# Attention and top-1 expert layer on one core: low halves and gating moved to VectorE, second-layer weight units cut by column parity, first expert loads on GpSimd's queue

## The chip, the cores and the metric

The kernel runs on 1 core of one Trainium2 chip. The metric is the device time of one execution in microseconds (us), as the median of several runs.

## The reference

For 8 batches of 448 tokens and 12 heads of 64 columns, sigmoid attention is computed. Its output, 3584 tokens by 768 columns, is the input of a layer of 8 experts of which each token takes one. All is float32.

```python
scores = scale * np.matmul(q, k.transpose(0, 1, 3, 2)) - np.log(S)
attn = 1.0 / (1.0 + np.exp(-scores))
x = np.matmul(attn, v)                    # per head; then tokens x 768
logits = x @ w_gate                       # 768 x 8
expert_idx = np.argmax(logits, axis=1)
gate_w = softmax(logits)[arange(N), expert_idx]
for e in range(E):
    mask = expert_idx == e
    h = np.maximum(x[mask] @ w1[e], 0.0)  # 768 x 1024
    out[mask] = gate_w[mask, None] * (h @ w2[e])   # 1024 x 768
```

## The kernel before

**Stages.** Attention runs over pairs of heads in 168 steps (`attention()`, L562). A step computes scores (`sc`, L522), their sigmoid on ScalarE (`at`, L509) and the product with the values (`av`, L536). From step 36 on, each step also runs 14 matmuls of the expert layer (`more`, L647): the generator `moe(b, wts)` (L192) yields after each matmul, so that attention and experts alternate on TensorE. A batch has 21 steps and 288 expert matmuls. When attention is done, some 300 expert matmuls are left; between them the kernel prepares a last stage.

**A batch and its expert.** For each batch the gate (`gate_a` to `gate_e`, L252 to L384) finds each token's expert and the expert that most of the batch's tokens chose, `ri`. `load_regs` (L386) reads `ri` into a register of SyncE, and `moe` sends the whole batch, 448 columns wide, through that one expert. Tokens with another expert are recorded in `recs` by four indirect DMAs on GpSimd's queue (L361), and are computed in the last stage, in items of up to 256 rows (`item`, L828), whose results overwrite those rows of the output.

**Split weights.** Each float32 factor is split in a high half (a rounded copy, made by ScalarE, L143) and a low half (factor minus high half, L144), and each product is made of three matmuls: high by high, high by low, low by high. `part_split(st, parts, eng)` (L141) makes both halves; `eng` makes the low one. For the batches that engine is GpSimd.

**Units and rings.** The first layer has 8 units per batch (`KF`), each 128 columns of w1, 128x768; a unit serves 18 matmuls. The second layer has 12 units (`NU`), each 128x512. Its output is made in three blocks `d` of 256 columns, and each block in two passes `t`, one for the even columns and one for the odd. A second-layer unit held two row blocks of w2 with all 256 columns, and the matmul took every second column of it as its weights (L223). So the four units of a block served pass 0, and again pass 1, and were given back one by one in pass 1. The ring of w2 units has 5 buffers, that of w1 units 3 (`RING`, L128). Raw weights come by DMA into a ring of 5 (`wst`, L162), all on SyncE's queue, which also loads q, k and most of v. One raw load of w2 (`w2_rows`, L133) holds four row blocks of 256 columns, that is two units.

**Order.** All of this is written in the order in which each engine gets it (`manual_schedule`), and each engine and each queue takes its instructions strictly in that order. `wts.ahead(n)` (L171) emits the splits up to unit n, and the raw loads that this allows. In the second layer it was called in pass 1 only, after every second row block (L233). After each pass VectorE transposes the pass's sum out of PSUM (`ob`, L237; two PSUM buffers, `ps_moe`); after both, GpSimd multiplies the block by the gates (L239), and its queue stores it by four DMAs (L244). `ob` has two buffers, which the last stage uses again for its `hf` (L900).

Of the kernel before, what the change touches and what calls it, by code (L numbers as in the profile page):

```python
# [19 lines left out]
P = 128  # L20
# [5 lines left out]
def tile_sigmoid_attention_top1_moe(  # L26
# [18 lines left out]
    nc = tc.nc  # L45
    B, H, S, D = q.shape
    NT, DM = out.shape
    E = w_gate.shape[1]
# [81 lines left out]
    def raw_view(st, n):  # L130
        return st.rearrange("p (t f) -> p t f", f=n)
# [9 lines left out]
    def part_split(st, parts, eng):  # L141
        hi, lo = parts
        nc.scalar.copy(hi, st)  # L143
        eng.tensor_tensor(lo, st, hi.bitcast(F32), op=ALU.subtract)  # L144

    class Weights:
# [9 lines left out]
        def load(self, n):  # L156
            while self.loaded < min(n, len(self.eregs) * self.LOADS):
                b, i = divmod(self.loaded, self.LOADS)
                ereg = self.eregs[b]()
                if ereg is None:  # L160
                    break
                st = wpool.tile([P, 1024], F32, tag="wst", bufs=RAWS_AHEAD, name=f"wst_{b}_{i}")  # L162
                if i < KF:
                    src = w1[bass.ds(ereg, 1), :, i * P : (i + 1) * P].rearrange("e (t p) f -> p (e t) f", p=P)
                    nc.sync.dma_start(raw_view(st[:, :DM], P), src)
                else:
                    w2_rows(ereg, i - KF, st)
                self.raw[self.loaded] = st
                self.loaded += 1

        def ahead(self, n):  # L171

            while True:
                b, i = divmod(self.split, self.PARTS)
                u = i - KF
                at = b * self.LOADS + (i if u < 0 else KF + u // 2)
                self.load(at + RAWS_AHEAD)
                if self.split >= n or at not in self.raw:
                    break
                st = self.raw[at]  # L180
                if u < 0:
                    parts = part_tiles("w1", DM, f"{b}_{i}")
                    part_split(st[:, :DM], parts, nc.gpsimd)
                else:
                    parts = part_tiles("w2", 512, f"{b}_{i}")
                    part_split(st[:, u % 2 * 512 : (u % 2 + 1) * 512], parts, nc.gpsimd)
                if u < 0 or u % 2:
                    del self.raw[at]
                self.parts[self.split] = parts
                self.split += 1  # L190

    def moe(b, wts):  # L192
# [25 lines left out]
        for d in range(ND):  # L218
            ob = opool.tile([P, NB, 32, 2], F32, tag="ob", name=f"ob_{b}_{d}")
            for t in range(2):  # L220
                ps = ps_moe.tile([P, 512], F32, tag="moe", name=f"ps2_{b}_{d}_{t}")
                for j in range(KF):
                    whi, wlo = (  # L223
                        x[:, j % 2 * DW : (j % 2 + 1) * DW].rearrange("p (m t) -> p t m", t=2)[:, t]
                        for x in wts.parts[w0 + KF + 4 * d + j // 2]
                    )
                    hh, hl = hts[j]
                    for n, (a, b_) in enumerate(((whi, hh), (whi, hl), (wlo, hh))):
                        nc.tensor.matmul(  # L229
                            ps[:, :S], a, b_, start=(j == 0 and n == 0), stop=(j == KF - 1 and n == 2)  # L230
                        )
                        yield
                    if t == 1 and j % 2:  # L233
                        wts.ahead(w0 + KF + min(NU, 4 * d + j // 2 + 6))
                    if d == ND - 1 and (t, j) in ((0, 1), (0, 5), (1, 1)):
                        wts.ahead(w0 + wts.PARTS + {(0, 1): 1, (0, 5): 2, (1, 1): 3}[t, j])
                nc.vector.transpose(ob[:, :, :, t], ps[:, :S].rearrange("p (j s) -> p j s", s=32))  # L237
            obv = ob.rearrange("p j s t -> p j (s t)")
            nc.gpsimd.tensor_tensor(  # L239
                obv, obv, gate_rows[b].unsqueeze(2).broadcast_to([P, NB, 2 * 32]), op=ALU.mult  # L240
            )
            for i in range(4):
# [143 lines left out]
    def load_regs(b):  # L386
        ri = gate_out[b]
        regs[b] = nc.sync.value_load(ri[0:1, 0:1], min_val=0, max_val=E - 1)

    KH = KD // 2  # L390
    xts = {}
# [170 lines left out]
    def attention():  # L562
# [31 lines left out]
        for s in range(N_ST + 11):  # L594
            u, i = divmod(s, ST)
            if s == 6:
                setup()
            if s == START - 1:
                wts.ahead(2)
            if s < ALONE:  # L600
                steps(s, 1, s - 1)
            elif i == 0:
# [360 lines left out]
```

## Time and profile before

| what | us |
|---|---|
| median of 3 runs | 889.35 (889.07 to 890.4) |
| the profiled execution | 887.08 |
| its span, first to last instruction | 885.1 |
| TensorE busy | 848.2 |
| VectorE, ScalarE, GpSimd busy | 300.1, 392.0, 410.3 |
| mean granted TensorE clock | 0.982 |

The busy time of an engine says little about an engine that others wait for only at some points. In the views of waits and groups, a row names the line, the engine, what is written and read, and how long the engine sat idle before it and for whom. "POOL" is GpSimd, "DVE" VectorE, "ACT" ScalarE, "PE" TensorE and "SPq" SyncE's queue. In the timeline a row has its start and its length; "x3" joins three instructions; the time in brackets is the idle time before it, with what ended it. Batches are counted from 0; the names `w2l_17` and the like in the orders below are numbered per batch: 0 to 7 are first-layer units, 8 to 19 second-layer units.

### The profile page before, as it was taken

How to read it: one execution, taken by the hardware profiler on the slowest of the kernel's cores; microseconds unless marked ns; L12 is line 12 of the kernel's file. 1: busy time of each engine (PE TensorE's matmuls, PEld its weight loads, DVE VectorE, ACT ScalarE, POOL GpSimd, SP SyncE). 2: the span in 40 equal slices, each digit the busy share in tenths (PEclk: the TensorE clock that was granted, in tenths of full speed). 3: DMA queues.
4: the chain of work that ended last, by engine and by line, in shares of the span. 5: the costliest groups of instructions: out<-in, count | busy, mean ns of one | idle time of the engine just before them, and what ended most of it. 6: DMA issues, size and time to landing. Idle time of an engine off the chain costs nothing.

```text
span 885.1 us, 15521 instructions
## 1 busy us (share of the span) xinstructions
PE 848.2 (96%) x5612; PEld 645.1 (73%) x5612; DVE 300.1 (34%) x679; ACT 392.0 (44%) x691; POOL 410.3 (46%) x377
## 2 busy tenths in 40 slices
PE   8998999999999999999989999899989998999986
PEld 6855678677687776677668677677767787899875
DVE  2453145123342235123422135022331135516354
ACT  4865543435433634444534534254335421234444
POOL 3114234744185326633464325724364448766340
PEclk8999999999999999999999999999999999899998
DMA  8788863675646844866446654668233424545614
GB/s 144 133 151 189 195 150 94 164 149 127 139 111 152 175 97 106 184 147 132 85 129 144 155 118 124 133 140 179 72 95 109 128 55 132 147 148 181 238 59 139
DMA packets 301929, 120.60 MB, mean 136 GB/s; under 512 B 211588, under 2 KB 296660, under 8 KB 301856
## 3 DMA queue, kind: packets, MB, share of 16 engines
q1 hardware_dynamic: 292512, 104.25, 50.1%
q0 software_dynamic: 7488, 14.93, 7.1%
q8 instruction: 44, 0.72, 0.4%
q10 hardware_dynamic: 1856, 0.46, 0.3%
q14 instruction: 29, 0.24, 0.1%
HBM read 97.55 MB, written 24.64 MB: 138 GB/s over the span
## 4 chain that ended last, share of the span: by engine, by line
PE 83%; issue 4%; DMA 4%; POOL 3%; DVE 2%; SPq 2%; ACT 1%; POOLq 0%; ACTq 0%; DVEq 0%
PE ps L208 27%; PE ps L229 23%; PE sc L522 13%; PE av L536 13%; PE ps L839 3%; PE psg L256 2%; POOL recs L361 1%; SPq L445 1%; DMA w2r<-in_moe_w_dram 1%; DMA first<-in_q_dram 1%; POOL w2l L144 1%; DMA out_dram<-ob 1%; DVE w1l_item L144 1%; SPq L408 1%; DMA wst<-in_moe_w_dram 0%
## 5 line engine op out<-in xcount | busy, mean ns | idle before, releaser
L509 ACT ACTIVATE at<-sc,bias_s 128x448 f32<-128x448 f32 x336 | 196.0, 636 | 198.8 <-PE sc L522 198.6
L144 POOL TENSOR_TENSOR w2l<-wst,w2h 128x512 fp32r<-128x512 f32 x96 | 121.5, 1291 | 161.8 <-ACT w2h L143 153.1
L522 PE MATMUL sc<-qt,kt 64*64 64x448 f32 x1344 | 177.0, 556 | 3.3 <-ACT at L509 2.5
L144 POOL TENSOR_TENSOR w1l<-wst,w1h 128x768 fp32r<-128x768 f32 x64 | 117.0, 1840 | 136.2 <-ACT w1h L143 123.1
L536 PE MATMUL av<-at,vn 64*64 64x448 f32 x1344 | 172.5, 544 | 0.0
L229 PE MATMUL ps<-hh,w2l 128*128 128x448 f32 x384 | 144.5, 376 | 12.2 <-POOL w2l L144 12.2
L208 PE MATMUL ps<-xh,w1l 128*128 128x448 f32 x384 | 142.1, 370 | 4.8 <-POOL w1l L144 4.8
L208 PE MATMUL ps<-xh,w1h 128*128 128x448 f32 x384 | 143.2, 373 | 0.0
L229 PE MATMUL ps<-hl,w2h 128*128 128x448 f32 x384 | 142.9, 372 | 0.0
L229 PE MATMUL ps<-hh,w2h 128*128 128x448 f32 x384 | 142.5, 371 | 0.0
L208 PE MATMUL ps<-xl,w1h 128*128 128x448 f32 x384 | 142.3, 370 | 0.0
L522 PEld LDWEIGHTS sc<-qt,kt 64*64 64x64 f32 x1344 | 77.8, 192 | 64.4 <-issue 50.2
L213 ACT ACTIVATE hh<-ps 128x448 fp32r<-128x448 f32 x64 | 35.1, 549 | 149.3 <-PE ps L208 149.3
L536 PEld LDWEIGHTS av<-at,vn 64*64 64x64 f32 x1344 | 55.6, 134 | 57.4 <-issue 55.1
L214 DVE SCALAR_TENSOR_TENSOR hl<-ps,hh 128x448 fp32r<-128x448 f32 x64 | 39.7, 620 | 166.5 <-ACT hh L213 166.5
L143 ACT CAST w2h<-wst 128x512 fp32r<-128x512 f32 x96 | 58.1, 624 | 80.3 <-PE ps L229 70.0
L229 PEld LDWEIGHTS ps<-hh,w2l 128*128 128x128 f32 x384 | 75.5, 197 | 24.7 <-POOL w2l L144 13.7
L208 PEld LDWEIGHTS ps<-xh,w1h 128*128 128x128 f32 x384 | 72.9, 190 | 16.6 <-issue 10.7
L208 PEld LDWEIGHTS ps<-xh,w1l 128*128 128x128 f32 x384 | 72.9, 190 | 12.9 <-POOL w1l L144 5.6
L229 PEld LDWEIGHTS ps<-hl,w2h 128*128 128x128 f32 x384 | 75.1, 196 | 9.2 <-issue 5.5
L208 PEld LDWEIGHTS ps<-xl,w1h 128*128 128x128 f32 x384 | 72.8, 190 | 8.8 <-issue 2.8
L229 PEld LDWEIGHTS ps<-hh,w2h 128*128 128x128 f32 x384 | 75.4, 196 | 3.5
(150 smaller groups left out, 817.8 us busy)
## 6 DMA issues: line engine op xcount, KB each, us to landing
wst<-in_moe_w_dram SPq DMA_DIRECT2D x64, 384.0 KB, 4.2
wst<-in_moe_w_dram SPq DMA_DIRECT2D x48, 512.0 KB, 4.1
x_tok<-xt SPq DMA_DIRECT2D x64, 168.0 KB, 3.9
out_dram<-ob POOLq DMA_DIRECT2D x96, 112.0 KB, 2.9
kn<-in_k_dram SPq DMA_DIRECT2D x184, 56.0 KB, 3.9
qn<-in_q_dram SPq DMA_DIRECT2D x184, 56.0 KB, 2.7
vn<-in_v_dram SPq DMA_DIRECT2D x76, 112.0 KB, 3.8
w1r<-in_moe_w_dram SPq DMA_DIRECT2D x12, 512.0 KB, 3.4
```

Of the source, the lines that this page charges most:

```text
L143: nc.scalar.copy(hi, st)
L144: eng.tensor_tensor(lo, st, hi.bitcast(F32), op=ALU.subtract)
L208: nc.tensor.matmul(ps[:, :S], a[:, ws], b_, start=(t == 0 and n == 0), stop=(t == KD - 1 and n == 2))
L213: nc.scalar.activation(hh[:, :S], ps[:, :S], AF.Relu)
L214: nc.vector.scalar_tensor_tensor(hl[:, :S], ps[:, :S], 0.0, hh[:, :S].bitcast(F32), op0=ALU.max, op1=ALU.subtract)
L229: nc.tensor.matmul(ps[:, :S], a, b_, start=(j == 0 and n == 0), stop=(j == KF - 1 and n == 2))
L256: nc.tensor.matmul(psg[: 2 * E, :S], wgs[:, t], xch[b, t][n], start=(t == 0 and n == 0), stop=(t == KD - 1 and n == 1),)
L361: put = nc.gpsimd.indirect_dma_start(out=recs, out_offset=bass.IndirectOffsetOnAxis(ap=si[:, c : c + 1], axis=0), in_=rec[:, c, :], in_off ...
L509: nc.scalar.activation(at, ps[:, :S], AF.Sigmoid, bias=bias_s, scale=SCALE)
L522: nc.tensor.matmul(ps[quarter(g, h), :S], ks, ops[g, "q"][OWN[h]], start=True, stop=True)
L536: nc.tensor.matmul(psv[g][OWN[h], :S], ops[g, "v"][rows, c, :], at[rows], start=(c == 0), stop=(c == KC - 1))
L839: nc.tensor.matmul(*a, **kw)
```

## The change

**Engines.** VectorE makes the low halves for the batches in place of GpSimd (64 of 128x768 and 96 of 128x512), and VectorE multiplies the 24 output blocks by the gates. GpSimd's queue still stores them.

**Units.** A second-layer unit now holds one column parity `t` of four row blocks. Its split reads every second column of the raw tile and writes them side by side; the matmul's weights are 128 adjacent columns. A unit serves 12 matmuls in a row and is then given back, so `ahead` is called after each unit, in both passes. Units of both parities read the same raw tile, so a raw tile is kept until pass 1's unit has read it (`oldest`).

**First batch.** GpSimd's queue reads the first expert's number into a register of its own and loads that batch's w1; and the splits of its first two units, which stood one step ahead of the first expert matmul (`if s == START - 1`), now stand at that matmul.

```diff
@@ load @@
                 if i < KF:
+                    eng, ereg = (nc.gpsimd, regs["first"]) if b == 0 else (nc.sync, ereg)
...
-                    nc.sync.dma_start(raw_view(st[:, :DM], P), src)
+                    eng.dma_start(raw_view(st[:, :DM], P), src)
@@ ahead @@
-                at = b * self.LOADS + (i if u < 0 else KF + u // 2)
-                self.load(at + RAWS_AHEAD)
+                if u < 0:
+                    at = oldest = b * self.LOADS + i
+                else:
+                    d, t, jh = u // 4, u // 2 % 2, u % 2
+                    at = b * self.LOADS + KF + 2 * d + jh
+                    oldest = at if t else at - jh
+                self.load(oldest + RAWS_AHEAD)
...
-                    part_split(st[:, :DM], parts, nc.gpsimd)
+                    part_split(st[:, :DM], parts, nc.vector)
                 else:
                     parts = part_tiles("w2", 512, f"{b}_{i}")
-                    part_split(st[:, u % 2 * 512 : (u % 2 + 1) * 512], parts, nc.gpsimd)
-                if u < 0 or u % 2:
+                    src = raw_view(st, DW).rearrange("p j (m t) -> p t j m", t=2)[:, t]
+                    part_split(src, [x.rearrange("p (j m) -> p j m", m=P) for x in parts], nc.vector)
+                if u < 0 or t:
                     del self.raw[at]
@@ moe, second layer @@
-                    whi, wlo = (
-                        x[:, j % 2 * DW : (j % 2 + 1) * DW].rearrange("p (m t) -> p t m", t=2)[:, t]
-                        for x in wts.parts[w0 + KF + 4 * d + j // 2]
-                    )
+                    u = 4 * d + 2 * t + j // 4
+                    whi, wlo = (x[:, j % 4 * P : (j % 4 + 1) * P] for x in wts.parts[w0 + KF + u])
...
-                    if t == 1 and j % 2:
-                        wts.ahead(w0 + KF + min(NU, 4 * d + j // 2 + 6))
+                    if j % 4 == 3:
+                        del wts.parts[w0 + KF + u]
+                        wts.ahead(w0 + KF + min(NU, u + 6))
...
-            nc.gpsimd.tensor_tensor(
+            nc.vector.tensor_tensor(
                 obv, obv, gate_rows[b].unsqueeze(2).broadcast_to([P, NB, 2 * 32]), op=ALU.mult
             )
@@ load_regs @@
+        if b == 0:
+            regs["first"] = nc.gpsimd.value_load(ri[0:1, 0:1], min_val=0, max_val=E - 1)
@@ attention @@
-            if s == START - 1:
-                wts.ahead(2)
```

Two places show how the order moves. The first is GpSimd's order in batch 3, before: between blocks `d` = 0 and 1 (`ob_0`, `ob_1`) it gates and stores a block, then records the gate's results of a later batch (`rec`, `recs`), and only then makes the low halves of units 17 to 19.

```order
L144 TENSOR_TENSOR w2l_16_4768<-wst_12_4404,w2h_16_4767 128x512
L239 TENSOR_TENSOR ob_0_4590<-ob_0_4590,gt_3990 128x896
L244 DMA out_dram<-ob_0_4590 32x14x64 x4
L357 IOTA rec_4916 128x4
L361 DMA recs<-rec_4916,si_4914 28672x2 x4
L144 TENSOR_TENSOR w2l_17_4939<-wst_12_4404,w2h_17_4938 128x512
L144 TENSOR_TENSOR w2l_18_4951<-wst_13_4497,w2h_18_4950 128x512
L144 TENSOR_TENSOR w2l_19_4961<-wst_13_4497,w2h_19_4960 128x512
```

After the change GpSimd's order holds none of these subtractions, and VectorE's order at the same place is this (`xl`, `xt` and `qt`, `kt` belong to attention; `pre` to `rec` are the gate's ranks):

```order
L245 TENSOR_TENSOR ob_0_4599<-ob_0_4599,gt_3999 128x896
L553 TENSOR_TENSOR xl_4848<-av_4651,xh_4847 128x448
L408 STREAM_TRANSPOSE xt_0_4851<-av_4651 128x14x32
L553 TENSOR_TENSOR xl_4854<-av_4654,xh_4853 128x448
L408 STREAM_TRANSPOSE xt_0_4851<-av_4654 128x14x32
L144 TENSOR_TENSOR w2l_17_4879<-wst_13_4510,w2h_17_4878 128x512
L501 STREAM_TRANSPOSE kt_4885<-kn_4516 128x448
L144 TENSOR_TENSOR w2l_18_4907<-wst_12_4413,w2h_18_4906 128x512
L243 STREAM_TRANSPOSE ob_1_4786<-ps_3_1_0_4787 128x448
```

So units 17 and 18 now stand ahead of the transpose of block 1's first pass, and no recording stands ahead of them; they were behind the recording.

The second place is ScalarE's order at the first expert matmul. Before, two high halves of w1 (`w1h`) stood ahead of the sigmoids of four attention steps (`at_0` to `at_3`):

```order
L509 ACTIVATE at_6_1075<-sc_6_1068,bias_s 128x448
L143 CAST w1h_0_1081<-wst_0_916 128x768
L143 CAST w1h_1_1087<-wst_1_918 128x768
L509 ACTIVATE at_0_1099<-sc_0_1093,bias_s 128x448
L509 ACTIVATE at_0_1101<-sc_0_1094,bias_s 128x448
L509 ACTIVATE at_1_1113<-sc_1_1107,bias_s 128x448
```

After the change they stand behind those sigmoids (`xh` is the high half of attention's output):

```order
L517 ACTIVATE at_1_1112<-sc_1_1105,bias_s 128x448
L552 CAST xh_1118<-av_975 128x448
L552 CAST xh_1123<-av_978 128x448
L517 ACTIVATE at_2_1135<-sc_2_1129,bias_s 128x448
L517 ACTIVATE at_2_1137<-sc_2_1130,bias_s 128x448
L517 ACTIVATE at_3_1145<-sc_3_1139,bias_s 128x448
L517 ACTIVATE at_3_1147<-sc_3_1140,bias_s 128x448
L143 CAST w1h_0_1161<-wst_0_925 128x768
L143 CAST w1h_1_1167<-wst_1_927 128x768
```

The two casts moved behind eight sigmoids and two other casts; on TensorE the order of the matmuls is the same.

## The prediction, made before the result

> **What bounds the kernel now.** I read the page's busy shares first, then TensorE's own waits, then the timeline and the windows around each wait. The busy row, and the three longest waits of TensorE (sum, times, longest):
>
> ```profile
> PE 848.2 (96%) x5612; PEld 645.1 (73%) x5612; DVE 300.1 (34%) x679; ACT 392.0 (44%) x691; POOL 410.3 (46%) x377
> ```
>
> ```profile
> PE ps L229 <- POOL w2l L144: 12.2, 4, 3.6
> PE ps L208 <- POOL w1l L144: 4.8, 2, 3.8
> PE sc L522 <- ACT at L509: 2.5, 1, 2.5
> ```
>
> TensorE is busy nearly always, so only its few waits can be won. The largest are six waits for GpSimd's low halves: 12.2 + 4.8 = 17.0 us. One of them in batch 3, on GpSimd, ScalarE and TensorE in turn:
>
> ```profile
> 446.75 1.04 POOL L361 DMA_INDIRECT recs<-rec,si  x1 [6.62 <-issue]
> ...
> 451.70 3.73 POOL L144 TENSOR_TENSOR w2l<-wst,w2h 128x512 fp32r<-128x512 f32 x3
> ```
>
> ```profile
> 446.43 0.62 ACT L143 CAST w2h<-wst 128x512 fp32r<-128x512 f32 x1 [0.61 <-PE ps L229]
> ```
>
> ```profile
> 448.82 0.36 PE L229 MATMUL ps<-hh,w2h 128*128 128x448 f32 x1
> 449.02 0.37 PE L229 MATMUL ps<-hl,w2h 128*128 128x448 f32 x1
> 453.03 0.47 PE L229 MATMUL ps<-hh,w2l 128*128 128x448 f32 x1 [3.65 <-POOL w2l L144]
> ...
> 454.63 0.57 PE L229 MATMUL ps<-hh,w2h 128*128 128x448 f32 x1
> 455.01 0.57 PE L229 MATMUL ps<-hl,w2h 128*128 128x448 f32 x1
> ```
>
> All three high halves are there at 447.05 (446.43 + 0.62), but GpSimd stands for 6.62 us, from 440.1 to 446.75, at the recording of the gate's results, issues four indirect DMAs, and starts the subtractions at 451.70. TensorE stops at 449.4 and goes on at 453.03. So the bound at this place is GpSimd's order, not its speed. And after the gap the matmuls start 0.38 apart (454.63, 455.01) instead of 0.20 (448.82, 449.02): the granted clock has fallen. Windows behind the four long gaps (columns: time, busy time of each engine, granted clock, DMA):
>
> ```profile
> 453.00:457.00 4.00, 3.97 (x14) 2.75 (x18) 0.82 (x2) 0.00 (x0) 4.00 (x3) 0.58 0.40 110
> 555.40:559.40 4.00, 3.98 (x14) 2.77 (x18) 0.18 (x1) 0.00 (x0) 3.71 (x4) 0.58 0.34 98
> 658.00:662.00 4.00, 4.00 (x18) 2.68 (x21) 1.35 (x3) 0.00 (x0) 3.71 (x5) 0.57 0.56 143
> 751.30:757.50 6.20, 6.19 (x17) 5.50 (x18) 5.94 (x4) 0.00 (x0) 5.90 (x5) 0.51 0.65 186
> ```
>
> **The change, part by part.** *The six waits: minus 17.0.* VectorE makes the low halves and no recording stands ahead of them; the 17.0 us go if VectorE is in time. Its price per operation is read from the same subtraction in the last stage at a moment when GpSimd rests, and from the 512-wide group; the gating's shape stands in GpSimd's row:
>
> ```profile
> 838.46 1.23 DVE L144 TENSOR_TENSOR w1l_item<-w1r,w1h_item 128x1024 fp32r<-128x1024 f32 x1 [0.25 <-ACT w1h_item L143]
> ```
>
> ```profile
> L144 DVE TENSOR_TENSOR w2l_r<-w2r,w2h_r 128x512 fp32r<-128x512 f32 x24 | 15.8, 687 | 12.8 <-ACT w2h_r L143 12.1 <-issue 0.5
> ```
>
> ```profile
> L239 POOL TENSOR_TENSOR ob<-ob,gt 128x896 f32<-128x896 f32 x24 | 41.6, 1732 | 35.2 <-DVE ob L237 35.2
> ```
>
> Between 0.69 (512) and 1.23 (1024) the 768-wide one takes some 0.96 and the gating (896) 1.1. Added to VectorE, in 8 batches of 8 and 12 units: 64 x 0.96 + 96 x 0.69 + 24 x 1.1 = 61 + 66 + 26 = 153 us, so 300 becomes some 450 of 885: half the span. What counts is lateness. A unit is split when the unit five before it is given back, so four units, 4 x 12 matmuls x 0.20 = 9.6 us without any attention between, lie ahead of its use; ScalarE 0.62 and VectorE 0.69 need 1.3 of that. The first layer's units have two units, 36 x 0.20 = 7.2 us. What is late next is the high half, and it was 2.3 us ahead of TensorE's stop (447.05 against 449.4). I take zero waits at these six places.
>
> Behind a waiting low half stand, on VectorE, attention's transposes and the transposes that free PSUM:
>
> ```profile
> L237 DVE STREAM_TRANSPOSE ob<-ps 128x448 f32<-128x448 f32 x48 | 30.9, 643 | 119.6 <-PE ps L229 91.8 <-issue 16.3 <-POOL w1l L144 11.2
> ```
>
> After a pass ends, high half (0.62), low half (0.69) and transpose (0.64) follow, 2.0 us. TensorE is back at that buffer after 24 x 0.20 = 4.8 us, or after 18 x 0.20 = 3.6 where the next batch's first layer follows. Covered, with 1.6 us to spare.
>
> *The clock behind them: minus 8.1.* Lost work is length times the missing clock: 4 x 0.42, 4 x 0.42, 4 x 0.43 and 6.2 x 0.49, that is 1.7 + 1.7 + 1.7 + 3.0 = 8.1 us. A short gap loses none, such as this one:
>
> ```profile
> 353.01 0.47 PE L229 MATMUL ps<-hh,w2l 128*128 128x448 f32 x1 [1.89 <-POOL w2l L144]
> ```
>
> Of the four waits for `w2l`, 1.89 and 3.65 are shown, so the other two share 12.2 - 5.5 = 6.7; of the two for `w1l`, one is 3.8 and the other 1.0.
>
> The Trainium skill, "TensorE: Matmul & The Clock Gate", section "What's actually happening", has the array run at half rate until a busy window of some 3.4 us is over: by that page the four would be worth 4 x 1.7 = 6.8 us as an estimate. The last window shows more, and the sum goes by the windows.
>
> *Strided reads: zero.* Splits now read every second column, in place of the matmuls' weights. The rows for bounds: strided and plain weight loads, and a ScalarE copy that writes with a stride of four beside a plain one.
>
> ```profile
> L229 PEld LDWEIGHTS ps<-hh,w2h 128*128 128x128 f32 x384 | 75.4, 196 | 3.5
> L208 PEld LDWEIGHTS ps<-xh,w1h 128*128 128x128 f32 x384 | 72.9, 190 | 16.6 <-issue 10.7
> L475 ACT COPY qt<-sc_first_q 128x448 f32<-128x448 f32 x2 | 1.9, 950 | 8.2 <-PE sc_first_q L469 8.2
> L213 ACT ACTIVATE hh<-ps 128x448 fp32r<-128x448 f32 x64 | 35.1, 549 | 149.3 <-PE ps L208 149.3
> ```
>
> The weight load is hidden (196 ns, and matmuls start 200 apart), so nothing is won there. The splits lie between 1.0 and 950/549 = 1.7 times their price; I take 1.0, since the stride of two is nearer to the weight load's. At 1.7 the chain above is 2.9 us, still under 3.6, and ScalarE gains 42 us of busy time and VectorE 46 off the path.
>
> *The first batch: plus 0.9, from minus 0.8 to plus 3.* The place before:
>
> ```profile
> 60.33 0.15 DVE L312 TENSOR_SCALAR ri<-cr 128x1 int32<-128x1 f32 x1
> ```
>
> ```profile
> 67.72 3.12 SPq L445 DMA_DIRECT2D qn<-in_q_dram  x4
> 71.92 3.88 SPq L165 DMA_DIRECT2D wst<-in_moe_w_dram  x5
> ```
>
> ```profile
> 72.20 1.16 ACT L509 ACTIVATE at<-sc,bias_s 128x448 f32<-128x448 f32 x2 [0.34 <-PE sc L522]
> 75.59 0.83 ACT L143 CAST w1h<-wst 128x768 fp32r<-128x768 f32 x1 [2.24 <-DMA wst<-in_moe_w_dram]
> ```
>
> ```profile
> 74.93 0.93 PE L536 MATMUL av<-at,vn 64*64 64x448 f32 x8
> 78.38 3.56 PE L522 MATMUL sc<-qt,kt 64*64 64x448 f32 x16 [2.52 <-ACT at L509]
> 81.87 0.47 PE L208 MATMUL ps<-xh,w1h 128*128 128x448 f32 x1
> ```
>
> The expert's number is there at 60.5, but SyncE issues loads of k and q until 70.84. ScalarE waits for the first w1 at 75.59, and the sigmoids behind it hold TensorE for 2.52. SyncE needs 1.1 us from there to the first load (70.84 to 71.92), 3.9 for five, and the first is in 3.7 after its issue (75.59). GpSimd's queue has nothing to do there, so by the same prices the loads start at 61.6 and are in by 71. Now the sigmoids don't wait: TensorE goes on at 75.7 with its last two score steps, until 77.4, ScalarE the eight sigmoids (1.16 a pair) and two casts until 79.7, then the first high half until 80.5, and VectorE the low half until 81.55. The third expert matmul starts at 81.6 instead of 82.4: 0.8 sooner. But TensorE has then been idle for 3.2 us, and gaps of 3.3 to 3.8 dropped the clock while the one of 1.89 did not. If it drops, 1.7 is lost: 1.7 - 0.8 = 0.9 slower, which I take. The plus 3 is for q and k loads that w1's traffic delays. On GpSimd's queue the five loads pass only the recording, which TensorE doesn't wait for; the other three wait there for a raw buffer, with only the first block's store behind them. SyncE's queue is rid of 3.9 us. Later, GpSimd's queue waits for VectorE's gating in place of its own, with only stores and recordings behind it.
>
> *The end: minus 1.0.* The last stage's second `hf` waits for a store of the last block:
>
> ```profile
> PE ph L885 <- ACT hf L901: 1.0, 1, 1.0
> ```
>
> ```profile
> 813.33 3.45 DVE L144 TENSOR_TENSOR w1l_item<-w1r,w1h_item 128x1024 fp32r<-128x1024 f32 x3
> ```
>
> ```profile
> 817.42 1.70 POOL L239 TENSOR_TENSOR ob<-ob,gt 128x896 f32<-128x896 f32 x1 [2.82 <-DVE ob L237]
> 819.41 2.54 POOL L244 DMA_DIRECT2D out_dram<-ob  x4 [0.29 <-POOL ob L239]
> ```
>
> ```profile
> 827.32 0.60 ACT L901 ACTIVATE hf<-ps 128x512 f32<-128x512 f32 x1 [3.91 <-DMA out_dram<-ob]
> ```
>
> Gating at 1.1 instead of 1.70 brings the store 0.6 us forward. The last transpose stood behind three subtractions until 816.78; units given back in both passes free the raw buffers for their loads sooner, so these end sooner too. I take TensorE's whole wait, 1.0.
>
> Sum: -17.0 - 8.1 + 0.9 - 1.0 = -25.2 us. The profiled execution took 887.08 us (span 885.1 and 1.98 around it), so 861.9; the median of the runs is 2.27 above it, 889.35, so **864.2**.
>
> **The rivals.** *VectorE takes GpSimd's place.* Its queue also waits for q and k loads and for the gate's matmuls; if these hold it past the 9.6 or 7.2 us of lead, TensorE waits again, at the same places. For it: the added half of VectorE's time. Against: lead is many times the work. Price: some 2 us at each of the six, without the clock's loss: 864.2 + 12 = 876.
>
> *Slower: strided splits hold PSUM.* High half, low half and transpose take 0.1 + 1.31k + 0.64, with k the price of the stride; TensorE waits from 4.8 us on, that is from k = 3.1. It eats the gain (25.2 us over 48 passes, 0.53 each) at k = 3.5, and at k = 4 costs 1.2 x 48 = 57 us: 864 + 57 = 921. The row above bounds k at 1.7 for twice that stride; so 3 in 100.
>
> *Stores and loads on GpSimd's queue are held by VectorE.* If a DMA of that queue can't be issued while VectorE works, the last store comes later by up to the three subtractions ahead of it: 3.4 us, and the 1.0 isn't won: 864.2 + 4.4 = 868.6. w1's first loads have 8 us to spare. The Trainium skill, "SBUF — State Buffer", section "SBUF: two separate sides", warns of this for VectorE operations in a two-port mode; it infers that a subtraction of two tiles does not do it. No row here shows such a hold.
>
> *The waits aren't on the path.* Then nothing moves: 889. Against: TensorE's rows before and after each gap are back to back.
>
> **How the numbers follow.** Forecast 0.77; VectorE late 0.10; the held queue 0.07; no change 0.02; slower 0.03; 0.01 for slower in a way not seen. The forecast's own range: with the start at -0.8, 862.5; with the start at +3 and nothing won at the end, 867.3. To 861 at the low end for a store that comes even sooner; to 873 at the high end, which takes in the held queue and part of late VectorE, with fewer than 2 in 10 left out. A difference of 0.2% (1.8 us) is about what a measurement of this kernel can tell. Faster by more than that: 0.94; within: 0.02; slower: 0.04.
>
> **What would show it.** Right: no wait of TensorE for a low half in batches 1 to 7, granted clock 1.00 from 340 us on to the last stage, and mean clock up from 0.982; the first w1 loads issued near 61.6; VectorE near 450 us busy. Wrong: waits of TensorE for `w2l`, `w1l` on VectorE, or for `ob`'s transposes; a high or low half of 512 columns that takes over 1.2 us; a gap at the first expert matmul over 5 us.

## The result, and the profile after

The changed kernel takes 865.12 us (median of 4 runs, 862.97 to 865.65); beside it the kernel before took 889.88 (889.07 to 891.27). The ratio is 0.9716, with a 95% interval of 0.9694 to 0.9737. The profiled execution took 865.44 us, with a span of 863.5 and a mean granted clock of 0.991 (before: 887.08, 885.1 and 0.982). The forecast was 864.2, so the time came out as predicted. But two terms of the sum were wrong in opposite directions, and the trace shows where.

The busy row of the page after:

```profile
PE 837.6 (97%) x5612; PEld 622.4 (72%) x5612; DVE 416.2 (48%) x863; ACT 396.3 (46%) x691; POOL 141.3 (16%) x201
```

GpSimd fell from 410.3 to 141.3 us, VectorE rose from 300.1 to 416.2. The longest waits of TensorE (sum, times, longest):

```profile
PE sc L530 <- DVE gt L389: 5.9, 1, 5.9
PE ph L891 <- ACT hf L907: 2.6, 2, 2.4
PE ps L215 <- ACT w1h L143: 2.2, 1, 2.2
```

All six waits for a low half are gone. The three longest that are left lie at the start and at the end of the program. Between them TensorE is without a gap and at full clock. Windows of the kernel after (columns: time, busy time of each engine in the order of the busy row, granted clock, DMA share, GB/s; a transfer's time counts in the window in which it starts, so the share of a short window can exceed 1):

```profile
400.00:500.00 100.00, 100.00 (x673) 73.02 (x675) 48.11 (x100) 45.58 (x82) 12.10 (x17) 1.00 0.62 140
700.00:780.00 80.00, 80.00 (x403) 71.31 (x403) 46.17 (x107) 23.89 (x42) 20.46 (x28) 1.00 0.50 136
```

and the same two of the kernel before:

```profile
400.00:500.00 100.00, 96.36 (x638) 70.47 (x631) 30.90 (x74) 43.62 (x78) 45.23 (x41) 0.98 0.58 127
700.00:780.00 80.00, 75.16 (x370) 65.42 (x369) 33.59 (x74) 21.77 (x38) 54.94 (x50) 0.96 0.41 114
```

The place of batch 3 that the prediction worked through, on GpSimd and then TensorE, after:

```profile
450.25 1.05 POOL L367 DMA_INDIRECT recs<-rec,si  x1 [9.08 <-issue]
```

```profile
459.33 0.36 PE L234 MATMUL ps<-hh,w2l 128*128 128x448 f32 x1
459.52 0.36 PE L234 MATMUL ps<-hh,w2h 128*128 128x448 f32 x1
459.72 0.37 PE L234 MATMUL ps<-hl,w2h 128*128 128x448 f32 x1
```

GpSimd stands at the recording as before (9.08 us), but nothing that TensorE needs is queued behind it, and the matmuls follow each other at 0.20 us.

To see where the time went, mark the start of the second batch's gate in each trace (the first matmul into `psg` there, in the middle of attention): 117.55 us before, 123.62 after. From that mark to the end the kernel takes 767.5 us before and 739.9 after: 27.6 us won. Up to the mark it takes 6.1 us more. And this hides some: the first gate's matmul into `pr`, which stands ahead of everything that was changed, came at 64.08 before and at 62.13 after. (In the versions below that leave this first stretch as it was, that matmul comes anywhere from 61.66 to 65.56.) Counted from `pr`, the start lost 8.0 us. The forecast for it was 0.9.

The place on GpSimd, SyncE's queue, VectorE and TensorE, after:

```profile
60.37 4.30 POOL L166 DMA_DIRECT2D wst<-in_moe_w_dram  x5 [12.22 <-DVE lm L335]
```

```profile
61.66 2.16 SPq L453 DMA_DIRECT2D qn<-in_q_dram  x4
63.86 10.46 SPq L453 DMA_DIRECT2D kn<-in_k_dram  x4
74.42 1.99 SPq L453 DMA_DIRECT2D qn<-in_q_dram  x4
```

```profile
75.50 0.65 DVE L501 STREAM_TRANSPOSE qt<-qn 128x448 f32<-128x448 f32 x1 [8.35 <-DMA qn<-in_q_dram]
76.07 0.14 DVE L389 COPY gt<-pg 128x16 f32<-128x16 f32 x1
```

```profile
76.26 1.02 PE L530 MATMUL sc<-qt,kt 64*64 64x448 f32 x2 [5.93 <-DVE gt L389]
...
86.26 0.74 PE L215 MATMUL ps<-xh,w1h 128*128 128x448 f32 x1 [2.23 <-ACT w1h L143]
86.80 0.57 PE L215 MATMUL ps<-xl,w1h 128*128 128x448 f32 x1
```

w1's loads set out at 60.37, near the forecast 61.6. But then four loads of k need 10.46 us on SyncE's queue instead of 2.04, and the q rows land up to 12.3 us after their issue (at most 3.1 before). VectorE stands 8.35 us at the transpose of q; behind it in its queue is the small copy `gt`, which frees the score bank, and TensorE waits for that 5.93 us. The wait's row names `gt`; the cause is two steps further back, a transfer. The 0.74 and 0.57 of the last two rows are matmuls at half clock. Two windows after show it, behind the gap of 5.93 us and behind that of 2.23:

```profile
76.00:80.00 4.00, 3.74 (x24) 1.44 (x28) 0.21 (x2) 0.96 (x2) 0.00 (x0) 0.58 0.45 96
86.00:90.00 4.00, 3.74 (x10) 2.98 (x11) 3.25 (x4) 1.67 (x3) 2.50 (x3) 0.57 0.78 113
```

The kernel before has one such stretch there, behind its gap of 2.52 us (the row of 78.38 in the prediction):

```profile
78.00:82.00 4.00, 3.62 (x17) 1.41 (x18) 1.64 (x4) 4.00 (x9) 2.09 (x2) 0.57 1.24 251
```

By these rows the 8.0 us are gaps of 5.93 and 2.23 in place of one of 2.52, 5.6 us more, and two stretches of half clock in place of one, 1.7 us more (4 x 0.43); the rest, some 0.7, isn't traced.

At the end, on ScalarE and GpSimd after:

```profile
806.84 0.60 ACT L907 ACTIVATE hf<-ps 128x512 f32<-128x512 f32 x1 [5.37 <-DMA out_dram<-ob]
```

```profile
796.23 2.51 POOL L250 DMA_DIRECT2D out_dram<-ob  x4 [6.11 <-DVE ob L245]
```

The last store is issued 0.3 us after VectorE's gating (794.84 + 1.09 = 795.93), but it takes up to 9.3 us to land, where it took 5.9 before.

### The profile page after: what moved, and what is told of

It reads as the page before. It is cut to its first block, busy times and chain, and to the rows that moved or that the text cites. A ratio compares the mean times of both kernels' runs of the same rounds, so it can differ in the third digit from the quotient of the medians.

```text
span 863.5 us, 15431 instructions
## 1 busy us (share of the span) xinstructions
PE 837.6 (97%) x5612; PEld 622.4 (72%) x5612; DVE 416.2 (48%) x863; ACT 396.3 (46%) x691; POOL 141.3 (16%) x201
## 4 chain that ended last, share of the span: by engine, by line
PE 89%; DMA 5%; SPq 2%; DVE 1%; issue 1%; ACT 1%; POOL 0%; POOLq 0%; ACTq 0%; DVEq 0%
PE ps L234 28%; PE ps L215 28%; PE sc L530 14%; PE av L544 13%; PE ps L845 3%; PE psg L262 2%; DMA qn<-in_q_dram 2%; SPq L453 1%; DMA out_dram<-ob 1%; DMA w2r<-in_moe_w_dram 1%; DMA first<-in_q_dram 1%; SPq L416 1%; ACT at L517 0%; PE pl L271 0%; PE ph L891 0%
## 5 line engine op out<-in xcount | busy, mean ns | idle before, releaser
L530 PE MATMUL sc<-qt,kt 64*64 64x448 f32 x1344 | 179.3, 552 | 6.9 <-DVE gt L389 5.9
L544 PE MATMUL av<-at,vn 64*64 64x448 f32 x1344 | 175.2, 542 | 0.0
L250 POOL DMA_DIRECT2D out_dram<-ob x96 | 61.1, 649 | 509.1 <-DVE ob L245 488.2
L143 ACT CAST w2h<-wst 128x512 fp32r<-128x512 f32 x96 | 61.8, 662 | 85.4 <-PE ps L234 75.4
L144 DVE TENSOR_TENSOR w2l<-wst,w2h 128x512 fp32r<-128x512 f32 x96 | 64.1, 684 | 49.4 <-ACT w2h L143 49.1
L553 DVE TENSOR_TENSOR xl<-av,xh 128x448 fp32r<-128x448 f32 x48 | 29.1, 605 | 116.1 <-ACT xh L552 116.1
L234 PEld LDWEIGHTS ps<-hh,w2l 128*128 128x128 f32 x384 | 72.3, 188 | 12.7 <-issue 7.4
L234 PEld LDWEIGHTS ps<-hl,w2h 128*128 128x128 f32 x384 | 72.2, 188 | 11.1 <-issue 5.5
```

The source lines that it names most:

```text
L234: nc.tensor.matmul(ps[:, :S], a, b_, start=(j == 0 and n == 0), stop=(j == KF - 1 and n == 2))
L250: nc.gpsimd.dma_start(out[b * S : (b + 1) * S, cols].rearrange("(j r) f -> r j f", r=32), obv[32 * i : 32 * (i + 1)])
L530: nc.tensor.matmul(ps[quarter(g, h), :S], ks, ops[g, "q"][OWN[h]], start=True, stop=True)
L544: nc.tensor.matmul(psv[g][OWN[h], :S], ops[g, "v"][rows, c, :], at[rows], start=(c == 0), stop=(c == KC - 1))
L553: nc.vector.tensor_sub(xl, pv[:, :S], xh.bitcast(F32))
```

## Experiments

The theory after the result: the gain comes from low halves that no longer stand behind GpSimd's recordings; the loss at the start comes from w1's 1.97 MB, which take the DMA engines' time from k and q. The rivals: the units' lead alone removes the waits; the start's loss comes from the later splits, from GpSimd's queue as such, or from VectorE.

**The three parts, one at a time.** *Engines only*, on the kernel before:

```diff
-                    part_split(st[:, :DM], parts, nc.gpsimd)
+                    part_split(st[:, :DM], parts, nc.vector)
...
-                    part_split(st[:, u % 2 * 512 : (u % 2 + 1) * 512], parts, nc.gpsimd)
+                    part_split(st[:, u % 2 * 512 : (u % 2 + 1) * 512], parts, nc.vector)
...
-            nc.gpsimd.tensor_tensor(
+            nc.vector.tensor_tensor(
                 obv, obv, gate_rows[b].unsqueeze(2).broadcast_to([P, NB, 2 * 32]), op=ALU.mult
```

> The kernel before with one part of the change alone: VectorE makes the low halves of the weights and the gating; units and the first batch as before. Theory, that TensorE waited because a low half stood on GpSimd behind a recording and issues of DMAs: the six waits for w2l and w1l of batches 1 to 7 are gone, the clock is 1.00 from 340 us to the last stage, and since the start isn't changed the time is at least as low as the changed kernel's, 856 to 862. Rival, that the low halves were late because units came too late for any engine (too little lead): the waits stay, now for VectorE, and the time falls by less than 10 us, to 880 to 889.

Measured: 857.88 us (856.53 to 859.14), ratio 0.9649 (0.9618 to 0.9680). TensorE's longest wait:

```profile
PE sc L522 <- ACT at L509: 2.8, 1, 2.8
```

The theory holds: no low half is waited for, and this part alone is faster than the whole change.

*Units only*: the changed kernel with `nc.gpsimd` again for low halves and gating, w1's first loads on SyncE, and `wts.ahead(2)` put back.

> The kernel before with another part alone: a second-layer unit holds one column parity of four row blocks and is given back after the pass that reads it; GpSimd still makes low halves and gating, the first batch loads as before. Theory (order on GpSimd): the recording still stands ahead of a low half, so most of the six waits stay; 884 to 892. Rival (lead): units given back in both passes put each low half early enough on any engine, the waits go, 860 to 868. If GpSimd is slow at strided reads (its low halves above 1.5 us each), it falls behind and the time is above 892 by either theory.

Measured: 868.72 us (866.98 to 871.26), ratio 0.9767 (0.9734 to 0.9800). TensorE's waits for low halves, and GpSimd at the recording of batch 3:

```profile
PE ps L215 <- POOL w1l L144: 6.2, 2, 4.5
```

```profile
438.66 1.32 POOL L144 TENSOR_TENSOR w2l<-wst,w2h 128x512 fp32r<-128x512 f32 x1 [2.08 <-ACT w2h L143]
440.43 1.31 POOL L144 TENSOR_TENSOR w2l<-wst,w2h 128x512 fp32r<-128x512 f32 x1 [0.46 <-ACT w2h L143]
441.69 0.13 POOL L363 IOTA rec<- 128x4 uint32 x1
444.46 1.04 POOL L367 DMA_INDIRECT recs<-rec,si  x1 [2.64 <-issue]
...
449.41 1.32 POOL L144 TENSOR_TENSOR w2l<-wst,w2h 128x512 fp32r<-128x512 f32 x1
```

The theory fails here, and the time lies just above the rival's range: all four waits for `w2l` are gone although GpSimd still makes them and the recording still stands in its queue. With units given back after each pass, two low halves are made ahead of the recording and one is left behind it; before, three were left behind it (the row of 451.70 in the prediction). Only waits in the first layer stay, 6.2 us. So there are two cures, each of which removes the second layer's waits alone, and their gains don't add.

*First batch only*, on the kernel before:

```diff
-                    nc.sync.dma_start(raw_view(st[:, :DM], P), src)
+                    eng.dma_start(raw_view(st[:, :DM], P), src)
...
-            if s == START - 1:
-                wts.ahead(2)
```

with `eng` and GpSimd's register as in the change.

> The kernel before with the third part alone: the first batch's w1 loads on GpSimd's queue, and the two splits ahead of the first expert matmul left to the expert's own place; low halves, gating and units as before. Theory (w1's traffic delays q's and k's): the score matmul waits some 6 us near 70 us, and the kernel is 6 to 10 us slower than before, 896 to 900. Rival (the start was lost by VectorE's new work, the part changes nothing alone): within 2 us of 889.9.

Measured: 894.04 us (892.29 to 896.68) against 888.50, ratio 1.0062 (1.0040 to 1.0084): 5.5 us slower, by less than the expected 6 to 10. The same wait is back, and the same queue is held:

```profile
PE sc L525 <- DVE gt L384: 5.2, 1, 5.2
```

```profile
65.20 9.02 SPq L448 DMA_DIRECT2D kn<-in_k_dram  x4
```

VectorE has none of its new work in this kernel, so VectorE is not the cause.

**The start.** *The changed kernel with w1's first loads on SyncE*:

```diff
-                    eng, ereg = (nc.gpsimd, regs["first"]) if b == 0 else (nc.sync, ereg)
+                    eng = nc.sync
```

> The changed kernel, but the first batch's five w1 loads go on SyncE's queue again; the splits still stand where the change put them (none ahead of the first expert matmul). Theory, that w1's five loads on GpSimd's queue hold up the k and q loads which SyncE issues at the same time: q's rows land before VectorE wants them, the 5.9 us wait of the score matmul for gt is gone with the half clock behind it, and the time falls by 6 to 8 us, to 857 to 859. Rival, that the splits' later place or something in GpSimd's own work cost the 8 us at the start: the wait of 5.9 us may go or stay, but the time stays within 2 us of 865.1.

Measured: 859.71 us (858.23 to 861.09), ratio 0.9661 (0.9630 to 0.9692). The wait for `gt` is gone, and with it 5.4 us; the expected 857 to 859 was just missed. The splits still come late, and TensorE waits at the first expert matmul:

```profile
81.58 0.47 PE L215 MATMUL ps<-xh,w1h 128*128 128x448 f32 x1 [2.66 <-ACT w1h L143]
```

```profile
82.00:83.00 1.00, 0.68 (x4) 0.41 (x3) 1.00 (x2) 1.00 (x2) 0.00 (x0) 1.00 0.70 111
...
84.00:85.00 1.00, 1.00 (x4) 0.87 (x4) 0.81 (x2) 0.00 (x0) 0.00 (x0) 0.50 0.70 181
...
86.00:87.00 1.00, 1.00 (x5) 0.93 (x4) 0.00 (x0) 0.00 (x0) 0.00 (x0) 0.71 0.68 112
```

These windows show the clock falling after a gap of only 2.66 us: full until 83, then half until some 86.4. From `pr` to the second gate's mark this version takes 54.0 us, the kernel before 53.5 and the changed kernel 61.5: without the early loads 7.5 of the 8.0 are back, with the splits as late as in the change.

*Two loads on GpSimd's queue, three on SyncE's*, in the changed kernel:

```diff
-                    eng, ereg = (nc.gpsimd, regs["first"]) if b == 0 else (nc.sync, ereg)
+                    eng, ereg = (nc.gpsimd, regs["first"]) if b == 0 and i < 2 else (nc.sync, ereg)
```

> The changed kernel with only the first two w1 loads (0.79 MB) on GpSimd's queue, the other three on SyncE's behind k and q. Theory of traffic: with k and q alone the DMA engines are 66% busy, so some 0.8 MB fits into what they have left over 8 us; the wait of 5.9 us falls under 1.5, the four k loads take SyncE under 5 us; the first expert matmul still waits 2.2 us for its high half, with the half clock behind it: 858 to 861. Rival, that any load on GpSimd's queue at that place stops SyncE's issues for its whole length: a wait of over 4 us stays, 863 to 866.

Measured: 859.07 us (858.39 to 860.02), ratio 0.9681 (0.9648 to 0.9714). The wait for `gt` is gone, the longest for `qt` is 0.9, and SyncE's four k loads take:

```profile
64.22 3.86 SPq L453 DMA_DIRECT2D kn<-in_k_dram  x4
```

*Five half loads on GpSimd's queue, the other halves on SyncE's*: as many transfers on GpSimd's queue as in the change, with half the bytes.

```diff
-                    eng.dma_start(raw_view(st[:, :DM], P), src)
+                    dst = raw_view(st[:, :DM], P)
+                    if b == 0:
+                        eng.dma_start(dst[:, : KD // 2], src[:, : KD // 2])
...
+                        nc.sync.dma_start(dst[:, KD // 2 :], again[:, KD // 2 :])
```

(`again` is the same rows by SyncE's register.)

> The changed kernel, with each of the five first w1 loads cut in two: half of its bytes (192 KB) go on GpSimd's queue, the other half on SyncE's, behind k and q. GpSimd's queue so carries five transfers as in the change, but 0.98 MB, near the two whole loads' 0.79. Theory of bytes: the four k loads take SyncE 3.5 to 6 us to issue (3.86 with two loads, 10.46 with five), the wait for gt is under 2.5 us, 858 to 862. Rival, of the number of transfers on GpSimd's queue: the k loads still take over 8 us, the wait is over 4.5 us, 863 to 867.

Measured: 857.08 us (856.21 to 858.21), ratio 0.9658 (0.9632 to 0.9685), a little under the expected range; no wait for `gt` or `qt` over 0.7 us, and:

```profile
64.40 3.69 SPq L459 DMA_DIRECT2D kn<-in_k_dram  x4
```

Bytes, then, and not the number of transfers: 0.79 MB cost SyncE 3.86 us, 0.98 MB 3.69, 1.97 MB 10.46. The queue rows say why (packets, MB, share of the 16 DMA engines). From 60 to 71 us before, and from 60 to 76 us after:

```profile
q1 hardware_dynamic: 7892, 1.32, 67.4%
```

```profile
q0 software_dynamic: 688, 1.97, 57.0%
q1 hardware_dynamic: 6424, 0.89, 41.1%
```

Before, SyncE's queue with k and q took 67.4% of 11 us, 7.4 us of all engines. w1 on GpSimd's queue takes 57.0% of 16 us, 9.1 us. Together that is, as an estimate, 16.5 us of work from 60 us on, done at 76.5; VectorE got q's rows at 75.5, and the engines were full (57.0 + 41.1 = 98%). The estimate is rough: the last four q loads, which are part of the 7.4, went out only from 74.42 on. The Trainium skill, "DMA: Bandwidth & Descriptors", section "Queues, rings and completion order", says that each DMA engine takes turns between the queues that have work for it; the trace agrees in that k and q slow down and don't stop (0.89 MB of theirs moved in those 16 us).

*w1's first loads on ScalarE's queue*, twice: with the expert's number read by ScalarE,

```diff
-                    eng, ereg = (nc.gpsimd, regs["first"]) if b == 0 else (nc.sync, ereg)
+                    eng, ereg = (nc.scalar, regs["first"]) if b == 0 else (nc.sync, ereg)
```

> The changed kernel, with the first batch's w1 loads issued from ScalarE's queue in place of GpSimd's, at the same place of the program. Theory of traffic (1.97 MB of w1 takes the DMA engines' time from the k and q loads, whichever queue it comes from): the four k loads that took SyncE 10.46 us to issue still take over 7, the score matmul still waits 3 to 6 us, 862 to 867. Rival, of the queue (what GpSimd's queue sends gets ahead of SyncE's small packets in a way that another queue's doesn't): the four k loads take under 5 us, no wait over 2 us for gt, 857 to 861. ScalarE's own time for the five issues (some 4 us) may show as a wait of TensorE for a sigmoid by either.

and from a fixed expert, which leaves out reading the first batch's expert:

```diff
-                    src = w1[bass.ds(ereg, 1), :, i * P : (i + 1) * P].rearrange("e (t p) f -> p (e t) f", p=P)
+                    src = w1[slice(0, 1) if b == 0 else bass.ds(ereg, 1), :, i * P : (i + 1) * P].rearrange("e (t p) f -> p (e t) f", p=P)
```

> The changed kernel, with the first batch's eight w1 loads on ScalarE's queue and from expert 0 always, so that ScalarE needn't read the expert's number first (the first batch's result is that of expert 0). The same bytes as in the change set out within some 5 us of the same moment. Theory of traffic alone: SyncE's four k loads take over 7 us and q lands 8 us or more after its issue. Rival, of the queue (packets of GpSimd's queue are some 2.9 KB, those of the other queues 512 B and less, and k and q's 128 B get one turn for each): k loads under 5 us, q lands within 7 us. The time is not the point: ScalarE's five issues hold the sigmoids some 4 us, 862 to 868.

Measured: 869.69 us (868.26 to 870.86), ratio 0.9798 (0.9765 to 0.9832), and 868.0 in one run. Neither answers its question. In both ScalarE began to issue only when SyncE had come to the last four of these q loads; here the second, on ScalarE's queue and SyncE's queue:

```profile
66.75 4.93 ACTq L166 DMA_DIRECT2D wst<-in_moe_w_dram  x5
```

```profile
64.52 2.04 SPq L451 DMA_DIRECT2D kn<-in_k_dram  x4
66.66 1.99 SPq L451 DMA_DIRECT2D qn<-in_q_dram  x4
```

ScalarE stood before that (why isn't traced), the sigmoids behind the loads came late, and TensorE waited 9.8 us. Most k and q loads were out before w1's. Of the four q loads that set out beside w1's the slowest took 7.3 us to land, where it was at most 3.1 before. So w1 delays q from this queue too; whether it would press k and q less than from GpSimd's is open.

**Do the units add anything, and what is the best version?** *The change without its first-batch part*: w1's first loads on SyncE and, in the attention loop,

```diff
+            if s == START - 1:
+                wts.ahead(2)
```

> The change without its whole first-batch part: VectorE's low halves and gating and the new units, with w1's first loads on SyncE and the two splits ahead of the first expert matmul as before. Theory, that either of the two parts already removes the waits, so that they don't add: within 2 us of the engines alone (857.9), 856 to 860. Rival, that the units add their lead to it: 850 to 855. Rival, that the units cost something of their own (strided copies, the last stage's loads that start sooner and slow the last store): 860 to 863, with the wait for hf at the end over 1 us.

Measured: 859.44 us (856.69 to 861.94), ratio 0.9671 (0.9637 to 0.9706). That is 1.6 above the engines alone (857.88), with ranges that overlap. The kernel before, taken beside each version, has medians from 887.06 to 889.88, so versions that lie 1 or 2 us apart are not told apart by their medians.

*Engines only, with two w1 loads on GpSimd's queue* (the first diff above, `i < 2` and GpSimd's register):

> A version to beat both: the kernel before with VectorE's low halves and gating (857.9 alone), the splits ahead of the first expert matmul kept, and the first two w1 loads on GpSimd's queue. Theory: the first two w1 are there before ScalarE wants them, so the 2.8 us wait of the scores for a sigmoid behind the first high half goes, no half clock at the first expert matmul, and k and q are hardly held: 854 to 856. Rival: what is won there is lost by k and q again: 857 to 861, with a wait for gt or qt over 1.5 us.

Measured: 856.09 us (855.12 to 857.05), ratio 0.9642 (0.9610 to 0.9675), just above the expected 854 to 856; no wait of TensorE for a sigmoid or for w1 is left at the start.

*The whole change with two w1 loads on GpSimd's queue and the two early splits put back* (`i < 2`, and `wts.ahead(2)` as above):

> The changed kernel with two w1 loads on GpSimd's queue, three on SyncE's, and the two splits ahead of the first expert matmul put back: it is the 856.09 us version (engines alone, two loads on GpSimd) with the new units added. Theory, that the units are worth nothing once VectorE makes the low halves: 855 to 858, no wait over 1 us ahead of 700 us. Rival, that the units cost at the end, where the last stage's loads come sooner and its second hf waits for a store: 858 to 860, with a wait for hf over 1 us. Rival, that the later splits, not the traffic, were the rest of the start's loss: over 858 with a half clock near 80 us.

Measured: 855.63 us (854.65 to 856.30), ratio 0.9635 (0.9610 to 0.9661): the lowest median here. Its first expert matmuls:

```profile
76.47 0.47 PE L215 MATMUL ps<-xh,w1h 128*128 128x448 f32 x1
...
76.97 0.37 PE L215 MATMUL ps<-xh,w1l 128*128 128x448 f32 x1
```

The third stands 15.3 us behind `pr` (61.66), where it stood 18.3 before (82.38 - 64.08) and 25.1 after (87.25 - 62.13). With the units 855.63, without them 856.09: once VectorE makes the low halves, the units are worth nothing that these runs can tell.

Four of these versions differ only in the place of the two splits and in the queue of the first two w1 loads. With all loads on SyncE's queue, late splits took 859.71 and early ones 859.44. With two loads on GpSimd's queue, late splits took 859.07 and early ones 855.63. So neither an early load nor an early split wins anything that shows alone; together they win some 3.4 to 4.1 us. The traces agree: from `pr` to the second gate's mark the four take 54.0, 54.7, 53.9 and 50.5 us. The gap ahead of the first expert work says why: it is 2.7 us for late splits, and 3.1 for early splits that wait for SyncE's loads; with two early loads it is 2.4 for late splits and none for early ones.

*Low halves on VectorE, gating on GpSimd*: the first two edits of the first diff, without the third.

> The kernel before with VectorE making the low halves alone; gating stays with GpSimd, units and first batch as before. Theory: the six waits come of low halves queued behind recordings and issues, so all six go and the clock stays 1.00 through the batches; what the gating adds is the end, where the second hf waits for the last store: 0.5 to 1.5 us more than with both (857.9), 858 to 860, with a wait for hf at the end of 0.4 to 1.5 us. Rival: GpSimd's gating and stores were a part of the six waits' cause, and VectorE's transposes now wait for an ob buffer: over 862, with waits of TensorE for a PSUM bank in the second layer.

Measured: 860.30 us (859.15 to 861.57), ratio 0.9694 (0.9667 to 0.9720), just above the expected range. No wait for a low half or a PSUM bank, and at the end:

```profile
PE ph L885 <- ACT hf L901: 0.9, 1, 0.9
```

With the gating on VectorE too, this wait is gone. From the second gate's mark on, this version takes 741.3 us and the engines alone 740.2, so some 1 of the 2.4 us between the two medians lies there, about the size of this wait. The rest lies ahead of the mark, where no block is gated yet (the first one is at 150.2 us). So gating on VectorE wins the end, as forecast, and nothing else that shows.

## Why the prediction was right, and where it was wrong

*Six waits, minus 17.0, and the clock, minus 8.1: right, and too small.* From the gate's mark to the end 27.6 us were won, while the end itself (below) lost some 1.5 in the profiled run (1.0 to 2.4); so some 29 stand against the forecast 25.1. A part of the difference is in how a wait is shown: at 449 us the starts of two matmuls lay 4.01 us apart (449.02 to 453.03), 3.81 more than usual, and the row shows 3.65. The rest of the 4 us isn't traced to rows.

*The cause given for it: half of the truth.* "The bound at this place is GpSimd's order" is shown by the engines alone. But the units alone remove the second layer's waits with the order left as it is. The prediction let the units cost something (strided reads) and gave them no gain; it should have asked, too, how far ahead of the recording they bring a low half.

*Strided reads, 0: right.* ScalarE's high half took 662 ns instead of 624, so k is 1.06, and VectorE's strided low half 684, as the unstrided one of the last stage (687). The rival of splits that hold PSUM needed k = 3.5.

*VectorE's prices: right.* 684, 951 and 1092 ns against 0.69, 0.96 and 1.1 us. Its sum was too high (450 against 416.2), for a reason told below.

*The first batch, plus 0.9, from minus 0.8 to plus 3: this is the step that failed.* It measured plus 8.0. The place of the error is one sentence, "The plus 3 is for q and k loads that w1's traffic delays": the mechanism was named, but its size was taken from no row, and put at the edge of the range. The queue rows before had the number: k and q alone took 67.4% of the DMA engines from 60 to 71 us, which leaves 3.6 us of their time, and from 72 to 79 us, when w1 came in,

```profile
q1 hardware_dynamic: 3327, 1.67, 88.9%
```

1.67 MB took 0.889 x 7 = 6.2 us, so w1's 1.97 MB need 7.3. That is twice what was to spare, so by this estimate k and q had to be late by some 4 us. And the start's chain was followed for w1 only: `qt` and `gt` on VectorE, which wait for q, were not in it. The other part of the term, late splits and a half clock at the first expert matmul, was seen and came so: a gap of 2.23 us with the half clock behind it. But the prediction charged the half clock to the change alone. The row of 78.38 that it shows, 16 score matmuls in 3.56 us where eight take 0.93, already ran at half clock (the window of 78 to 82 above). By the prediction's own prices the two cancel, and the term without w1's traffic should have been minus 0.8. The first w1 loads were issued at 60.37, against 61.6 forecast.

*The end, minus 1.0: right in the mechanism, not in the profiled run.* Without the gating on VectorE the wait is 0.9, with it none; but with the new units it is 0.2 to 0.8 in the seven other versions that have VectorE's gating, and 2.6 (2.4 of it in one wait) in the changed kernel's profiled run, where the store took 9.3 us to land. In that stretch, 796 to 808 us, the DMA share was 0.99 and before, 818 to 830, 1.02; so full engines alone don't tell why this store landed later. That is left open.

*The rivals.* VectorE late: no, it is waited for at none of the six places. A held queue on GpSimd: not seen; the last store is issued 0.3 us after its data. Waits not on the path: no. The sum gave 861.9 for the profiled time, and the profiled run took 865.44, 3.5 more: 7.1 at the start and 2.5 at the end, less some 4 in the middle and less the 2.0 by which its first stretch happened to be ahead. The median of the runs stands 0.3 below the profiled run this time, not 2.3 above it, and so 864.2 comes as near to 865.12 as it does. The direction and most of the gain were foreseen with their mechanism; that the sum came within 1 us is luck.

## What to carry to other kernels

An earlier load isn't free because its queue is: read the share of the DMA engines at the new moment, and add up the engine time of all that must land there. When a wait's row names a small copy, look at what stands ahead of that copy in its engine's queue. And where a change has several parts, run each alone: here two of three did the same, and the third cost 5.5 us. An early load pays only if the work that waits for it moves too.

## What was not expected of the hardware

The granted clock fell to half for some 3.4 us after gaps of 2.23 and 2.66 us (83.0 to 86.4 in the version with w1 on SyncE). The prediction knew only of drops behind gaps of 3.3 us and more, and of one gap of 1.89 without; it had overlooked the drop behind the gap of 2.52. The Trainium skill, "TensorE: Matmul & The Clock Gate", section "What's actually happening", gives an idle window of about 3.4 us ahead of the half clock; here less was enough. But the length of a gap alone doesn't decide. With the engines alone, a gap of 2.82 us cost no clock:

```profile
76.34 2.22 PE L522 MATMUL sc<-qt,kt 64*64 64x448 f32 x14 [2.82 <-ACT at L509]
```

```profile
76.00:80.00 4.00, 3.66 (x22) 2.30 (x23) 2.43 (x5) 4.00 (x9) 0.00 (x0) 1.00 1.24 252
```

In the change without its first-batch part, a gap of 1.77 us in the last stage did:

```profile
823.21 0.40 PE L845 MATMUL ps<-w2l_r,h 128*128 128x256 f32 x1 [1.77 <-DVE w2l_r L144]
```

```profile
823.00:827.00 4.00, 3.79 (x19) 3.79 (x20) 2.12 (x5) 1.68 (x3) 0.51 (x1) 0.57 0.00 0
```

In the traces here, every gap of 3.1 us and more from the first gate on had the half clock behind it; of the gaps between 1.77 and 2.82 us some had it and some hadn't. What decides there is open.

VectorE stood still inside some of its short operations as long as GpSimd worked. Two places of the kernel before, GpSimd's row and then VectorE's:

```profile
729.00 1.70 POOL L239 TENSOR_TENSOR ob<-ob,gt 128x896 f32<-128x896 f32 x1
```

```profile
729.38 1.35 DVE L313 TENSOR_SCALAR ce<-ce,cr 128x8 f32<-128x8 f32 x1
```

```profile
754.74 1.70 POOL L239 TENSOR_TENSOR ob<-ob,gt 128x896 f32<-128x896 f32 x1
```

```profile
L706 DVE TENSOR_TENSOR ends<-ends,xo 128x1 f32<-128x1 f32 x1 | 8.0, 7999 | 0.0
```

The first ends at 730.73, with GpSimd's gating (730.70); the second runs from 748.5, when GpSimd is issuing stores, to 756.5, over three low halves and a gating of GpSimd, which ends at 756.44. After, the same two take 0.22 us (mean of eight) and 0.16. All of VectorE's older instructions, their lengths added up, fell from 322.8 us to 296.8; with the units alone, where GpSimd still subtracts, they stay at 327.9. These 26 us are most of the 34 by which the sum was forecast too high; in the rest, records of neighbouring instructions overlap, so that busy times don't add. The Trainium skill, "SBUF — State Buffer", section "SBUF: two separate sides", describes such a hold: one of the two engines has a shared port pair for a whole instruction and the other blocks. These rows agree; the prediction had weighed the rule only the other way round, for VectorE's work against GpSimd's queue.
